# Interleaving the row loads of the next batch with the DMA transposes of the present one

## The chip, the cores and the metric

The kernel runs on one core of one Trainium2 chip. The metric is the device time of one execution in microseconds (us), as a median of several runs. A run over 1.5% above the fastest of the same kernel counts as slow, the others as fast, and only fast runs are compared.

Engines are called PE (TensorE), PEld (TensorE's weight loads), DVE (VectorE), ACT (ScalarE), POOL (GpSimd) and SP (SyncE) in the profile. SPq is SyncE's queue of DMA issues. L373 is line 373 of the kernel's source; most operations go through one helper, so the tile names tell more than the line numbers.

## The reference, cut to what matters

```python
# q, k, v: (8, 8, 576, 64) float32: 8 batches, 8 heads, 576 tokens; s: (8, 8, 576)
scores = (q @ k^T) / 8 + min(-(cum_i - cum_j), 0)      # cum = cumsum(max(s, 0)); causal
x  = softmax(scores) @ v            # -> (4608, 512): 8 heads x 64 are the model dimension
xn = x / sqrt(mean(x^2) + 1e-6) * rms_g
out = (silu(xn @ w_gate) * (xn @ w_val)) @ w_out       # 512 -> 1536 -> 512
```

q and k are drawn as 0.1 × normal. A dot product of 64 terms is then about 0.1 × 0.1 × 8 = 0.08, and a score about 0.01.

## The kernel before

The work goes in nine chunks `c` of 512 tokens. In chunk c, TensorE does the first two FFN products (12 groups of 4 matmuls each with `wg_sb` and `wv_sb`), the attention of batch b = c + 1, and the last FFN product (48 matmuls with `wout_sb`, 10.4 us). Meanwhile rows of K, Q and V for batch c + 2 are loaded.

From batch 2 on, K and Q take this way: a row load of 128 tokens × 8 heads × 64 (256 KB) into `k_nat` or `q_nat`, a cast to bf16 on VectorE (`k_bf`, `q_bf`), and a DMA transpose into `KT` or `QT`. `k_nat`, `q_nat`, `v_nat`, `k_bf` and `q_bf` exist once. SyncE issues the row loads, the transposes, and the stores of the output, all in one queue, in order.

The order on every engine is decided when the kernel is built, by a list scheduler inside it (`Plan`). Each operation has a key (smaller goes first), a planned duration and its dependences. A DMA also has planned times for its transfer. Nothing of this runs on the chip; but every constant in it can move instructions. The loads are held back by one rule:

```python
# Plan.schedule(): when may operation o start on engine e?
can = []
for r, o in cand:                      # r: when its inputs are ready, in planned time
    # ... [cut: PSUM banks, the DMAs of GpSimd]
    if o.dma and e == "sp":
        r = max(r, self.dma_free - 3.0)    # at most 3 us of planned DMA work ahead, from ALL queues
    can.append((o.key, o.n, r, o))
# ... [cut: the candidate with the smallest key among those ready goes next]
if o.dma:
    begin = max(self.dma_free, s + o.us + o.lags[0])
    self.dma_free = begin + o.dma
    o.done = self.dma_free + o.lags[1]
```

The loads, the casts with the transposes, the output, and the loop that gives the keys:

```python
def load_rows(dst, src, b, eng, key):
    ops = []
    for sc in range(NB):               # NB = 5 blocks of 128 tokens, the last of 64
        n = 128 if sc < 4 else 64
        ops.append(I(eng, "dma_start", 0.88 if eng == "pool" else 0.4, key=key,
                     dma=1.28 * n / 128, lags=(1.2, 1.2 if b < 2 else 4.2),
                     out=dst[0:n, sc], in_=src[b, :, sc * 128 : sc * 128 + n, :].rearrange(
                         "h p d -> p h d")))
    return ops

def prep_cast(b, which, key):
    src, dst = ((k_nat, k_bf), (q_nat, q_bf))[which]
    out = (KT, QT)[which][b % 2]
    for sc in range(NB):
        n = 128 if sc < 4 else 64
        I("dve", "tensor_copy", 0.34, key=key + sc, out=dst[0:n, sc], in_=src[0:n, sc])
        I("sp", "dma_start_transpose", 1.27, key=key + sc, dma=0.65, lags=(0.5, 2.7),
          out=out[:, :, sc * 128 : sc * 128 + n], in_=dst[0:n, sc])

# in ffn2(c): O is the finished PSUM bank, osb a ring of NOSB = 3 buffers
    o = nxt("osb", osb)
    I("act", "activation", 0.6, ..., out=o, in_=O, func=AF.Copy, scale=0.5)
    I("sp", "dma_start", 0.4, key=key, dma=0.72, out=out[...], in_=o)

for c in range(NCH):
    K = PER * c                        # PER = 36
    # ... [cut: FFN1 groups of chunk c]
    b = c + 1
    # ... [cut: batches 0 and 1 take another way]
        for w in range(2):
            prep_cast(b, w, K - 14)
    # ...
    if b + 1 < B:
        n = b + 1
        for o in load_rows(k_nat, k, n, "sp", K + 16) + load_rows(q_nat, q, n, "sp", K + 16):
            ...
        lv = load_rows(v_nat[n % len(v_nat)], v, n, "sp", K + 16)
    ffn2(c, K + STEP * 96, STEP)
    attention(b, K + 1, 2.6, 2 if b > 3 else 4)
```

So one batch of loads stands in SyncE's order as five K, five Q and five V, with no transpose between them. `x_blk`, the normed output of attention, is also transposed by DMA (into `xnT`) from batch 3 on.

Of the kernel before, what the change touches and what calls it, by code (L numbers as in the profile page):

```python
# [75 lines left out]
class Plan:  # L76
# [59 lines left out]
    def schedule(self):  # L136
        ops = self.ops
        for o in ops:
            o.succ = []
        left = {}  # L140
        for o in ops:
            left[o.n] = len(o.preds)
            for p in o.preds:
                ops[p].succ.append(o)
        free = {}
        table = {}
        pool = {}
        self.dma_free = 0.0
        order = []
        held = [[0.0, None] for _ in self.banks]  # L150

        def ready(o):
            t = 0.0
            for p, raw in o.preds.items():
                q = ops[p]
                if q.eng == o.eng and not q.dma:
                    t = max(t, q.done if raw and o.eng != "pe" else q.start)
                else:
                    t = max(t, q.done + self.HOP)
            return t  # L160

        def room(o):
            group, cap, n = o.takes[0].group, o.takes[0].cap, len(o.takes)
            for t in sorted(f for f, _ in held if f is not None):
                free = sum(1 for f, _ in held if f is not None and f <= t)
                busy = sum(1 for f, g in held if g == group and (f is None or f > t))
                if free >= n and busy + n <= cap:
                    return t
            return None

        lanes = [0.0] * self.LANES

        def add(o):
            pool.setdefault(o.eng, []).append((ready(o), o))

        for o in ops:
            if not left[o.n]:
                add(o)
        while any(pool.values()):
            best = None  # L180
            for e, cand in pool.items():
                f = free.get(e, 0.8)
                can = []
                for r, o in cand:
                    if o.takes:
                        t = room(o)
                        if t is None:
                            continue
                        r = max(r, t)
                    if o.dma and e == "pool":  # L190
                        r = max(r, lanes[0] + self.HOP)
                    if o.dma and e == "sp":
                        r = max(r, self.dma_free - 3.0)
                    can.append((o.key, o.n, r, o))
                if not can:
                    continue
                t = max(f, min(x[2] for x in can))
                k = min((x for x in can if x[2] <= t + 0.02), key=lambda x: x[:2])
                if e in ("dve", "act", "pool"):
                    soon = [x for x in can if x[:2] < k[:2] and x[2] < t + self.AHEAD * k[3].us]  # L200
                    if soon:
                        k = min(soon, key=lambda x: x[2])
                s = max(f, k[2])
                if best is None or s < best[0]:
                    best = (s, e, k[3], f)
            s, e, o, f = best
            pool[e] = [(r, q) for r, q in pool[e] if q is not o]
            o.wait = s - f
            if o.kind is not None:
                if table.get(e) not in (None, o.kind):  # L210
                    s += self.TABLE
                table[e] = o.kind
            o.start = s
            free[e] = s + o.us
            o.done = s + o.us + o.lat
            if o.dma:
                begin = max(self.dma_free, s + o.us + o.lags[0])
                self.dma_free = begin + o.dma
                o.done = self.dma_free + o.lags[1]
                if e == "pool":  # L220
                    lanes[:] = lanes[1:] + [o.done]
            for bank in o.takes:
                i = min((i for i, (t, _) in enumerate(held) if t is not None),
                        key=lambda i: held[i][0])
                bank.phys = i
                held[i][:] = [None, bank.group]
            for bank in o.uses:
                bank.left -= 1
                if not bank.left:
                    held[bank.phys][0] = max(u.done for u in bank.users) + self.HOP  # L230
            order.append(o)
            for q in o.succ:
                left[q.n] -= 1
                if not left[q.n]:
                    add(q)
        assert len(order) == len(ops)
        self.order = order
        return order
# [7 lines left out]
def kernel(  # L246
# [25 lines left out]
    NB = 5  # L272
# [10 lines left out]
    NS = 3  # L283
    NOSB = 3
    NRUN = 2
    NTWO = 2
    NPE = 3

# [101 lines left out]
    def small_bank():  # L390
        return bank("small", 2)
# [6 lines left out]

    def load_runs(b, which, h0, h1, key):
        p0 = KP * which  # L400
        return I("pool", "dma_start", 0.8, key=key, dma=(4.0, 3.45)[b] * (h1 - h0) / 8, lags=(0.9, 1.3),
                 out=raw[b][p0 : p0 + KP, h0:h1, :, :].rearrange("p h c d -> p h (c d)"),
                 in_=(k, q)[which][b, h0:h1, :, :].rearrange("h (p c) d -> p h (c d)", c=KC))

    def load_rows(dst, src, b, eng, key):
        ops = []
        for sc in range(NB):
            n = 128 if sc < 4 else 64
            ops.append(I(eng, "dma_start", 0.88 if eng == "pool" else 0.4, key=key,
                         dma=1.28 * n / 128,  # L410
                         lags=(1.2, 1.2 if b < 2 else 4.2),
                         out=dst[0:n, sc], in_=src[b, :, sc * 128 : sc * 128 + n, :].rearrange(
                             "h p d -> p h d")))
        return ops

    def load_w(which, lo, hi, key):
        if which == 2:
            return I("pool", "dma_start", 0.84, key=key, dma=9.6 * (hi - lo) / 12,
                     out=wout_sb[:, lo:hi, :],
                     in_=moe_w_out[lo * 128 : hi * 128, :].rearrange("(fc p) d -> p fc d", p=128))  # L420
        dst, src = ((wg_sb, moe_w_gate), (wv_sb, moe_w_val))[which]
        return I("pool", "dma_start", 0.76, key=key, dma=8.9 * (hi - lo) / DF,
                 out=dst[:, :, lo:hi],
                 in_=src[:, lo:hi].rearrange("(cc p) f -> p cc f", p=128))

# [11 lines left out]
        else:  # L437
            I("act", "activation", 0.57, key=key, out=o, in_=i, func=AF.Copy)

    def prep_cast(b, which, key):  # L440
        src, dst = ((k_nat, k_bf), (q_nat, q_bf))[which]
        out = (KT, QT)[which][b % 2]
        for sc in range(NB):
            n = 128 if sc < 4 else 64
            I("dve", "tensor_copy", 0.34, key=key + sc, out=dst[0:n, sc], in_=src[0:n, sc])
            I("sp", "dma_start_transpose", 1.27, key=key + sc, dma=0.65, lags=(0.5, 2.7),
              out=out[:, :, sc * 128 : sc * 128 + n], in_=dst[0:n, sc])

    def prep_norm(b, which, i, key):
        n = 128 if i < 2 else 64  # L450
# [156 lines left out]
    def att_out(b, tb, key):  # L607
        x = x_blk[b % 2][:, tb, :]
        if b >= NPE:
# [1 line left out]
            I("dve", "scalar_tensor_tensor", 0.66, key=key, out=x, in0=x,  # L611
              scalar=al[b % 2][:, 1, tb : tb + 1], in1=gB, op0=ALU.mult, op1=ALU.mult)
            c0 = b * S + tb * 128
            I("sp", "dma_start_transpose", 1.27, key=key - 3, dma=0.65, lags=(0.5, 2.7),
              out=xnT[:, :, c0 : c0 + 128 - p0], in_=x_blk[b % 2][p0:128, tb, :])
            return
        I("act", "activation", 0.5, key=key, out=x, in_=x, func=AF.Copy,
# [51 lines left out]
    def ffn2(c, key, step):  # L669
        t0 = c * DM  # L670
        for tb in range(4):
            O = bank("ffn", 6)
            for f in range(0, FB, 2):
# [3 lines left out]
            o = nxt("osb", osb)  # L677
            I("act", "activation", 0.6, key=key + step * (tb * FB + FB), out=o, in_=O,
              func=AF.Copy, scale=0.5)
            I("sp", "dma_start", 0.4, key=key, dma=0.72,  # L680
              out=out[t0 + tb * 128 : t0 + (tb + 1) * 128, :], in_=o)

    whole = [(0, DM, fb) for fb in range(FB)]
# [36 lines left out]
    for hp in range(HP):  # L720
        prep_transpose(0, 0, hp, -80 + hp, "dve")
        prep_transpose(0, 1, hp, -80 + hp, "act")
    gp_ = small_bank()
    mms(0.1, [(gp_[:, 0:CC], g4, ident_F[0:CC, 0:CC], True, True, True)], key=-75)
    I("dve", "tensor_copy", 0.1, key=-75, out=g_sb, in_=gp_[:, 0:CC])
    prep_w(0, "act", -70)
# [14 lines left out]
    for c in range(NCH):  # L741
# [5 lines left out]
        if b < B:  # L747
# [2 lines left out]
                    prep_transpose(b, 0, hp, K + hp, "dve")  # L750
                    prep_transpose(b, 1, hp, K + hp, "act")
            else:
                for w in range(2):
                    prep_cast(b, w, K - 14)
            if b < NRUN:
                raw_norm(b, K + 18)
            else:
                for i in range(3):
                    for w in range(2):
                        prep_norm(b, w, i, K + 30)  # L760
            prep_w(b, "pool", K - 10)
            vops = [prep_v(b, sc, "pool", K - 8 + sc) for sc in range(NB)]
        if b + 1 < B:
            n = b + 1
            for o in load_rows(k_nat, k, n, "sp", K + 16) + load_rows(q_nat, q, n, "sp", K + 16):
                if n == NRUN:
                    R.after(o, *vops)
            lv = load_rows(v_nat[n % len(v_nat)], v, n, "sp", K + 16)
            if n == NRUN:
                R.after(gl, *lv)  # L770

        if c == B - 1:
            check_decay(K + 10)
            check_all(K + 20)
# [171 lines left out]
```

## Time and profile before

| | before |
|---|---|
| median (range) | 377.04 us (375.39 to 378.92; 3 runs) |
| span of the profiled run | 373.1 us |
| TensorE busy | 341.8 us |
| TensorE idle in 120 to 264 us | 10.94 us |
| one period, first K load to first K load | 39.6 us |

The head of the profile page of the kernel before gives the span, the busy time of each engine (share of the span, instructions) and, in part 4, which engine held the chain of work that ended last:

```profile
span 373.1 us, 7766 instructions
...
PE 341.8 (92%) x2907; PEld 207.6 (56%) x2934; DVE 251.6 (67%) x486; ACT 230.4 (62%) x469; POOL 127.8 (34%) x211
...
PE 62%; DMA 12%; DVE 9%; POOL 5%; SPq 4%; ACT 3%; issue 3%; DVEq 0%; ACTq 0%; POOLq 0%
```

TensorE is the busiest engine, but only 62% of the chain passes over it; a fifth passes over DMA, SyncE's queue and GpSimd. So waits for data are left, and the next question is where. The windows of the kernel before show each stretch of 36 us: its length, the busy time of each engine, the granted clock, the DMA share and the rate in GB/s.

```profile
120.00:156.00 36.00, 33.14 (x302) 23.61 (x301) 26.20 (x48) 22.85 (x49) 15.09 (x23) 0.95 0.89 161
156.00:192.00 36.00, 33.97 (x308) 23.05 (x308) 27.06 (x52) 22.95 (x51) 13.77 (x21) 1.00 0.91 162
192.00:228.00 36.00, 32.92 (x233) 16.19 (x236) 28.20 (x55) 24.02 (x51) 14.22 (x23) 1.00 0.88 163
228.00:264.00 36.00, 33.02 (x236) 16.02 (x240) 28.04 (x54) 22.29 (x48) 14.07 (x21) 1.00 0.85 168
```

TensorE is busy 133.06 of these 144 us. This is the stretch to look at: in the 72 us before it TensorE is idle 1.8 us, and in the 72 us after it 1.2 us. Its waits in this stretch (what it waited for: us in all, times, longest) name two causes:

```profile
PE psb L373 <- DMA QTa<-q_bf: 2.2, 1, 2.2
PE pse L373 <- DVE u_sbc L356: 1.7, 1, 1.7
PE psa L373 <- DVE u_sbc L356: 1.7, 1, 1.7
PE psf L373 <- DMA QTb<-q_bf: 1.6, 1, 1.6
```

Twice TensorE waits for a transpose of Q. Twice it waits for `u_sbc`, an FFN intermediate that VectorE makes. That second wait looks like a slow VectorE and is not. VectorE's timeline of the kernel before (start, duration, instruction, in brackets the idle time before it and its releaser) shows the first of the two:

```profile
209.73 0.66 DVE L356 CAST q_bf<-q_nat 128x512 bf16<-128x512 f32 x1 [1.51 <-DMA q_nat<-in_q_dram]
210.31 0.67 DVE L356 SCALAR_TENSOR_TENSOR u_sbc<-T_sbc,psa 128x512 bf16<-128x512 f32 x1
```

VectorE stood 1.51 us in front of a cast whose row load had not landed, and `u_sbc`, the next in its order, came behind it. TensorE's next matmul then shows 1.74 us idle, put down to `u_sbc`. The other such wait looks the same: VectorE stood 1.30 us in front of a `q_bf` cast at 249.41 us, and `u_sbc` came behind it. Both kinds of wait are therefore late K and Q rows. SyncE's timeline of the kernel before shows why they are late:

```profile
199.57 4.39 SPq L356 DMA_DIRECT2D k_nat<-in_k_dram  x5
204.01 6.49 SPq L356 DMA_DIRECT2D q_nat<-in_q_dram  x5
210.60 5.59 SPq L356 DMA_DIRECT2D v_nata<-in_v_dram  x5
216.28 2.57 SPq L356 DMA_TRANSPOSE xnT<-x_blkb  x2
218.94 1.22 SPq L356 DMA_TRANSPOSE KTa<-k_bf  x1
220.21 1.26 SPq L356 DMA_TRANSPOSE QTa<-q_bf  x1
```

Fifteen loads hold the queue for 16.5 us, 1.1 us each on average, then come the transposes at 1.2 to 1.3 us each. During the loads the share of busy DMA engines was 0.88 to 1.22, during the transposes 0.65 to 0.72. (The share is the time of the packets that start in a stretch over that of 16 engines, so it can pass 1.)

### The profile page before, as it was taken

How to read it: one execution, taken by the hardware profiler on the slowest of the kernel's cores; microseconds unless marked ns; L12 is line 12 of the kernel's file. 1: busy time of each engine (PE TensorE's matmuls, PEld its weight loads, DVE VectorE, ACT ScalarE, POOL GpSimd, SP SyncE). 2: the span in 40 equal slices, each digit the busy share in tenths (PEclk: the TensorE clock that was granted, in tenths of full speed). 3: DMA queues.
4: the chain of work that ended last, by engine and by line, in shares of the span. 5: the costliest groups of instructions: out<-in, count | busy, mean ns of one | idle time of the engine just before them, and what ended most of it. 6: DMA issues, size and time to landing. Idle time of an engine off the chain costs nothing.

```text
span 373.1 us, 7766 instructions
## 1 busy us (share of the span) xinstructions
PE 341.8 (92%) x2907; PEld 207.6 (56%) x2934; DVE 251.6 (67%) x486; ACT 230.4 (62%) x469; POOL 127.8 (34%) x211
## 2 busy tenths in 40 slices
PE   3869999999999997999979799979999999999993
PEld 3558775788577864787435444444445444444441
DVE  6478946797937895588837893879388638806830
ACT  3959698888769825874767547863687533313321
POOL 8976452504361544134613370345123200000000
PEclk9999999999999999899999999999999999999999
DMA  8999997977985997699758986699650170020012
GB/s 125 215 226 208 193 184 164 162 176 153 200 192 116 190 179 132 179 156 198 133 128 183 198 151 115 167 203 174 114 148 2 30 149 0 0 87 29 0 43 78
DMA packets 138356, 51.13 MB, mean 137 GB/s; under 512 B 127300, under 2 KB 132936, under 8 KB 138312
## 3 DMA queue, kind: packets, MB, share of 16 engines
q1 hardware_dynamic: 131688, 41.13, 55.8%
q0 software_dynamic: 6624, 9.44, 14.4%
q8 instruction: 25, 0.41, 0.5%
q14 instruction: 19, 0.16, 0.2%
HBM read 38.16 MB, written 9.44 MB: 128 GB/s over the span
## 4 chain that ended last, share of the span: by engine, by line
PE 62%; DMA 12%; DVE 9%; POOL 5%; SPq 4%; ACT 3%; issue 3%; DVEq 0%; ACTq 0%; POOLq 0%
PE psc L373 9%; PE psb L373 8%; PE psd L373 8%; PE psg L373 8%; PE psh L373 7%; PE psa L373 7%; PE psf L373 7%; PE pse L373 6%; DMA v_nata<-in_v_dram 5%; SPq L356 4%; DVE Hs L356 2%; DMA QTb<-q_bf 2%; DMA out_dram<-osbb 2%; DMA q_nat<-in_q_dram 1%; DMA k_nat<-in_k_dram 1%
## 5 line engine op out<-in xcount | busy, mean ns | idle before, releaser
L373 PEld LDWEIGHTS <-wv_sb 128*128 128x128 bf16 x624 | 60.7, 98 | 39.5 <-issue 7.2
L373 PEld LDWEIGHTS <-wg_sb 128*128 128x128 bf16 x624 | 58.6, 98 | 32.5 <-issue 5.1
L373 PEld LDWEIGHTS <-Hs 128*128 128x128 bf16 x432 | 41.3, 98 | 49.9 <-DVE Hs L356 2.1
L356 POOL TENSOR_TENSOR vwb<-v_nata,wT 128x512 bf16<-128x512 f32 (+1 forms) x20 | 21.1, 1073 | 12.2 <-DMA v_nata<-in_v_dram 11.9
L356 POOL TENSOR_SCALAR_AFFINE_SELECT Ea<-Ea 128x512 bf16<-128x512 bf16 x8 | 5.1, 644 | 56.0 <-ACT Ea L356 56.0
L356 ACT ACTIVATE sq_scr<-x_blka 128x512 bf16<-128x512 bf16 x19 | 12.0, 632 | 15.9 <-DVE x_blka L356 15.6
L356 DVE CAST q_bf<-q_nat 128x512 bf16<-128x512 f32 (+1 forms) x30 | 18.4, 621 | 3.7 <-DMA q_nat<-in_q_dram 3.7
L373 PE MATMUL psf<-xnT,wv_sb 128*128 128x256 bf16 (+1 forms) x116 | 20.6, 313 | 0.2
L356 ACT ACTIVATE sq_scr<-x_blkb 128x512 bf16<-128x512 bf16 x20 | 12.6, 630 | 13.1 <-DVE x_blkb L356 12.6
L356 POOL TENSOR_TENSOR vwa<-v_nata,wT 128x512 bf16<-128x512 f32 (+1 forms) x15 | 16.2, 1094 | 9.5 <-DMA v_nata<-in_v_dram 9.3
L356 DVE CAST k_bf<-k_nat 128x512 bf16<-128x512 f32 (+1 forms) x30 | 15.1, 515 | 5.2 <-DMA k_nat<-in_k_dram 5.2
L373 PE MATMUL psc<-wout_sb,Hs 128*128 128x512 bf16 x69 | 17.0, 379 | 0.9 <-DVE Hs L356 0.7
L373 PE MATMUL psd<-xnT,wg_sb 128*128 128x256 bf16 (+1 forms) x95 | 17.5, 316 | 0.1
L373 PE MATMUL pse<-xnT,wg_sb 128*128 128x256 bf16 (+1 forms) x102 | 17.3, 304 | 0.1
L373 PE MATMUL psh<-wout_sb,Hs 128*128 128x512 bf16 x70 | 16.6, 379 | 0.5 <-DVE Hs L356 0.4
L373 PE MATMUL psg<-wout_sb,Hs 128*128 128x512 bf16 x70 | 16.6, 379 | 0.1
L356 ACT ACTIVATE sq_scr<-q_bf 128x1024 bf16<-128x1024 bf16 (+1 forms) x18 | 16.5, 916 | 0.2
L373 PE MATMUL psc<-xnT,wg_sb 128*128 128x256 bf16 (+1 forms) x83 | 14.9, 316 | 1.8 <-DVE xnT L356 1.5
L373 PE MATMUL psb<-xnT,wg_sb 128*128 128x256 bf16 (+1 forms) x95 | 16.3, 308 | 0.1
L356 ACT ACTIVATE sq_scr<-k_bf 128x1024 bf16<-128x1024 bf16 (+1 forms) x18 | 16.3, 908 | 0.0
L356 DVE SCALAR_TENSOR_TENSOR x_blkb<-x_blkb,alb,gB 128x512 bf16<-128x512 bf16 x15 | 12.1, 859 | 5.0 <-POOL alb L356 5.0
L373 PE MATMUL psa<-xnT,wv_sb 128*128 128x256 bf16 (+1 forms) x75 | 13.4, 311 | 1.9 <-DVE u_sbc L356 1.7
(456 smaller groups left out, 859.6 us busy)
## 6 DMA issues: line engine op xcount, KB each, us to landing
k_nat<-in_k_dram SPq DMA_DIRECT2D x24, 256.0 KB, 4.7
q_nat<-in_q_dram SPq DMA_DIRECT2D x24, 256.0 KB, 5.8
v_nata<-in_v_dram SPq DMA_DIRECT2D x24, 256.0 KB, 5.1
out_dram<-osba SPq DMA_DIRECT2D x12, 256.0 KB, 2.3
out_dram<-osbb SPq DMA_DIRECT2D x12, 256.0 KB, 2.4
out_dram<-osbc SPq DMA_DIRECT2D x12, 256.0 KB, 2.4
v_nata<-in_v_dram POOLq DMA_DIRECT2D x8, 256.0 KB, 11.0
wg_sb<-in_moe_w_gate_dram POOLq DMA_DIRECT2D x2, 768.0 KB, 12.9
```

The costliest lines, as they stand in the source:

```text
L356: o = R.add(eng, us, lambda: f(**{n: real(a) for n, a in kw.items()}), outs, ins, key=key, lat=LAT[eng], kind=kind, dma=dma, name=outs[0]. ...
L373: nc.tensor.matmul(out, lhsT=lhsT, rhs=rhs, start=st, stop=sp)
```

## The change

The intent is to spread the loads: the pair of loads of K and Q for block sc of the next batch gets the key of the transposes of block sc + LEAD of the present one. By then the casts of block sc have freed that part of `k_nat` and `q_nat`. DMA engines then have loads to move while SyncE issues transposes. V follows after. The rule that holds back SyncE's DMAs now looks at SyncE's own DMAs only. The planned durations were measured again. The core of the diff:

```diff
@@ Plan.schedule
+        sp_free = 0.0
                     if o.dma and e == "sp":
-                        r = max(r, self.dma_free - 3.0)
+                        r = max(r, sp_free - 2.0)
 ...
+                if e == "sp":
+                    sp_free = self.dma_free
@@ constants
+    LEAD = 1
+    MARGIN = 3.0
-dma=(4.0, 3.45)[b] ... 0.4, dma=1.28 * n / 128      (row loads: issue, transfer)
+dma=(3.95, 3.35)[b] ... 0.45, dma=1.2 * n / 128
-dma=9.6 ... dma=8.9                                 (weights)
+dma=8.0 ... dma=7.8
-"dma_start_transpose", 1.27 ... "dma_start", 0.4, dma=0.72   (transposes, output stores)
+"dma_start_transpose", 1.31 ... "dma_start", 0.62, dma=0.75
@@ prep_cast: K and Q of one block together
-    for sc in range(NB):
-        (cast, transpose of one tensor; called for K, then for Q)
+    for sc in range(NB):
+        for src, dst, out in ((k_nat, k_bf, KT[b % 2]), (q_nat, q_bf, QT[b % 2])):
+            (cast, transpose)
@@ main loop
-            for o in load_rows(k_nat, k, n, "sp", K + 16) + load_rows(q_nat, q, n, "sp", K + 16):
-                if n == NRUN:
-                    R.after(o, *vops)
-            lv = load_rows(v_nat[n % len(v_nat)], v, n, "sp", K + 16)
+            K2 = K - 14 + LEAD
+            for sc in range(NB):
+                for dst, src in ((k_nat, k), (q_nat, q)):
+                    o = load_row(dst, src, n, sc, "sp", K2 + sc)
+                    if n == NRUN:
+                        R.after(o, *vops)
+            lv = [load_row(v_nat[n % len(v_nat)], v, n, sc, "sp", K2 + 6 + sc) for sc in range(NB)]
 ... [cut: prep_norm's keys, K + 30 -> K + 20 + 2 * i; another PSUM group for one small transpose]
```

(The lines of constants are abridged: the numbers are those of the diff, the code around them is left out.)

More of the change, by code (lines that the diff above doesn't have):

```diff
@@ L400, in load_runs, with load_row @@
         p0 = KP * which
-        return I("pool", "dma_start", 0.8, key=key, dma=(4.0, 3.45)[b] * (h1 - h0) / 8, lags=(0.9, 1.3),
+        return I("pool", "dma_start", 0.8, key=key, dma=(3.95, 3.35)[b] * (h1 - h0) / 8, lags=(0.9, 1.3),
                  out=raw[b][p0 : p0 + KP, h0:h1, :, :].rearrange("p h c d -> p h (c d)"),
                  in_=(k, q)[which][b, h0:h1, :, :].rearrange("h (p c) d -> p h (c d)", c=KC))
-    def load_rows(dst, src, b, eng, key):
-        ops = []
-        for sc in range(NB):
-            n = 128 if sc < 4 else 64
-            ops.append(I(eng, "dma_start", 0.88 if eng == "pool" else 0.4, key=key,
-                         dma=1.28 * n / 128,
-                         lags=(1.2, 1.2 if b < 2 else 4.2),
-                         out=dst[0:n, sc], in_=src[b, :, sc * 128 : sc * 128 + n, :].rearrange(
-                             "h p d -> p h d")))
-        return ops
+    def load_row(dst, src, b, sc, eng, key):
+        n = 128 if sc < 4 else 64
+        return I(eng, "dma_start", 0.88 if eng == "pool" else 0.45, key=key, dma=(1.08 if eng == "pool" else 1.2) * n / 128,
+                 lags=(1.2, 1.2 if b < NRUN else MARGIN + 1.2), out=dst[0:n, sc],
+                 in_=src[b, :, sc * 128 : sc * 128 + n, :].rearrange("h p d -> p h d"))
+    def load_rows(dst, src, b, eng, key):
+        return [load_row(dst, src, b, sc, eng, key) for sc in range(NB)]
     def load_w(which, lo, hi, key):
         if which == 2:
-            return I("pool", "dma_start", 0.84, key=key, dma=9.6 * (hi - lo) / 12,
+            return I("pool", "dma_start", 0.84, key=key, dma=8.0 * (hi - lo) / 12,
                      out=wout_sb[:, lo:hi, :],
@@ L421, in load_w @@
         dst, src = ((wg_sb, moe_w_gate), (wv_sb, moe_w_val))[which]
-        return I("pool", "dma_start", 0.76, key=key, dma=8.9 * (hi - lo) / DF,
+        return I("pool", "dma_start", 0.76, key=key, dma=7.8 * (hi - lo) / DF,
                  out=dst[:, :, lo:hi],
@@ L438, in prep_transpose, with prep_cast @@
             I("act", "activation", 0.57, key=key, out=o, in_=i, func=AF.Copy)
-    def prep_cast(b, which, key):
-        src, dst = ((k_nat, k_bf), (q_nat, q_bf))[which]
-        out = (KT, QT)[which][b % 2]
+    def prep_cast(b, key):
         for sc in range(NB):
             n = 128 if sc < 4 else 64
-            I("dve", "tensor_copy", 0.34, key=key + sc, out=dst[0:n, sc], in_=src[0:n, sc])
-            I("sp", "dma_start_transpose", 1.27, key=key + sc, dma=0.65, lags=(0.5, 2.7),
-              out=out[:, :, sc * 128 : sc * 128 + n], in_=dst[0:n, sc])
+            for src, dst, out in ((k_nat, k_bf, KT[b % 2]), (q_nat, q_bf, QT[b % 2])):
+                I("dve", "tensor_copy", 0.34, key=key + sc, out=dst[0:n, sc], in_=src[0:n, sc])
+                I("sp", "dma_start_transpose", 1.31, key=key + sc, dma=0.65,
+                  lags=(0.5, 0.9 + 0.6 * MARGIN),
+                  out=out[:, :, sc * 128 : sc * 128 + n], in_=dst[0:n, sc])
     def prep_norm(b, which, i, key):
@@ L613, in att_out @@
             c0 = b * S + tb * 128
-            I("sp", "dma_start_transpose", 1.27, key=key - 3, dma=0.65, lags=(0.5, 2.7),
+            I("sp", "dma_start_transpose", 1.31, key=key - 3, dma=0.65, lags=(0.5, 0.9 + 0.6 * MARGIN),
               out=xnT[:, :, c0 : c0 + 128 - p0], in_=x_blk[b % 2][p0:128, tb, :])
@@ L679, in ffn2 @@
               func=AF.Copy, scale=0.5)
-            I("sp", "dma_start", 0.4, key=key, dma=0.72,
+            I("sp", "dma_start", 0.62, key=key, dma=0.75,
               out=out[t0 + tb * 128 : t0 + (tb + 1) * 128, :], in_=o)
@@ L722 @@
         prep_transpose(0, 1, hp, -80 + hp, "act")
-    gp_ = small_bank()
+    gp_ = bank("g", 1)
     mms(0.1, [(gp_[:, 0:CC], g4, ident_F[0:CC, 0:CC], True, True, True)], key=-75)
@@ L752 @@
             else:
-                for w in range(2):
-                    prep_cast(b, w, K - 14)
+                prep_cast(b, K - 14)
             if b < NRUN:
@@ L759 @@
                     for w in range(2):
-                        prep_norm(b, w, i, K + 30)
+                        prep_norm(b, w, i, K + 20 + 2 * i)
             prep_w(b, "pool", K - 10)
```

## The prediction

> **What bounds it now.** TensorE: 341.8 of 373.1 us busy, 62% of the chain of waits. In the middle, batches 3 to 6, a second loop is as long: SyncE's queue. The timeline of SyncE shows the five K loads starting at 120.36, 160.01, 199.57 and 239.18 us: one batch takes 39.6 us, with hardly a gap. At 199.57 to 239.18 it spends 16.5 us on 15 row loads (back to back[...]), 19 us on 15 transposes (1.22 to 1.27 us each) and 2 to 3 us on output stores. TensorE is busy only 36.4 to 37.3 us of those 39.6 (windows by batch). DMA engines are loaded unevenly: share 0.88 to 1.22 while rows load, 0.65 to 0.72 while transposes go.
>
> TensorE's idle time in 120–264 us is 11.0 us. Its waits name the cause: 2.2 and 1.6 us for the transposes of Q at 147 and 188; twice 1.7 us for u_sb at 209 and 249. The second kind is also late loads: just before, VectorE stands 1.5 us in front of a cast that waits for a q_nat load, with u_sb behind it. GpSimd waits 3.6 us for v_nata at 212. After the 2.2 us stall some matmul groups take 1.6 to 1.9 us, not 1.04: 1.4 us more.
>
> **What the change does.** Same bytes, same transfers, same arithmetic. A pair of row loads follows the transposes of its block, so DMA fills the time in which SyncE issues transposes (two take 2.5 us), and the solid 11 us of K and Q loads ahead of V disappears. Issue of a load without a wait is about 0.4 us; one batch should hold SyncE about 15×1.26 + 15×0.45 + 2.5 = 28 us instead of 39.6 (estimate from these durations). V starts right after the last transpose instead of 11 us later. Casts spread out in VectorE's order. The new constants of the planner also move part of attention later, into the second FFN matmul of some chunks.
>
> The Trainium skill ("DMA: Bandwidth & Descriptors", Issuing engines are not separate DMA queues) says that all DMAs end on the same 16 engines and interleave. So bandwidth isn't gained: about 0.87×39.6 = 34.5 us of DMA work stays per batch. At a 37.5 us period that is a share of 0.92, so landings of transposes should lengthen, from 2.5 us to perhaps 3.5, and part of the gain goes back.
>
> **On the critical path.** Removable: 11.0 us of idle in 120–264, plus 1.4 us of slow clock. I expect about two thirds: 8.5 us. Start (11 us idle before 48, from first loads and set-up), 48–120 (1.9 us idle) and the last 75 us (FFN alone, store tail) stay within 1 us. 377.0 − 8.5 = **368.5 us**, range **362 to 376**. Faster by over 2%: 0.55; within 2%: 0.41; slower: 0.04.
>
> **Right if:** TensorE's busy time stays near 340 to 343 while its idle in 120–264 falls from 11 to 3–5 us; the period of K loads falls to about 37 to 38 us; waits of TensorE on the Q transposes and of VectorE on q_nat (3.5 us) nearly vanish; SyncE has free time in each batch; DMA share is even, about 0.9; transposes land later than 2.5 us.
>
> **Wrong if:** DMA is the true limit of the middle and the period stays at 39; or in-order SyncE now makes a transpose wait behind a load whose buffer isn't free, so attention starts late; or the moved attention leaves xnT late at the start of a chunk (waits of TensorE on xnT, DVE x_blk); or the new order of the first 60 us costs some us.

## The result, and the profile after

The ratios in this document are the mean time of one kernel's fast runs over that of the other's of the same rounds, so they are not quite the ratio of the medians quoted beside them.

| | before | after |
|---|---|---|
| median (range), same chip | 376.86 us (375.39 to 378.92; 4 runs) | 363.19 us (362.05 to 363.79; 4 runs) |
| ratio, 95% interval | | 0.963 (0.958 to 0.968): faster |
| span of the profiled run | 373.1 us | 360.4 us |
| TensorE busy | 341.8 us | 340.6 us |
| TensorE idle in 120 to 264 us | 10.94 us | 2.19 us |
| period in this stretch (before: first K load to first K load; after: first V load to first V load) | 39.6 us | 37.9 to 38.3 us |

The gain of the medians is 13.7 us. The head of the page and the chain by engine of the kernel after:

```profile
span 360.4 us, 7813 instructions
...
PE 340.6 (95%) x2934; PEld 207.1 (57%) x2934; DVE 251.3 (70%) x486; ACT 230.9 (64%) x469; POOL 129.0 (36%) x211
...
PE 76%; DVE 10%; ACT 4%; POOL 3%; DMA 3%; issue 2%; SPq 0%; DVEq 0%; ACTq 0%; POOLq 0%
```

The work is the same, but DMA fell from 12% to 3% of the chain and SyncE's queue from 4% to 0%. The windows of the kernel after, same columns as before:

```profile
120.00:156.00 36.00, 34.85 (x340) 25.70 (x339) 28.47 (x57) 28.35 (x62) 15.79 (x24) 1.00 0.97 175
156.00:192.00 36.00, 35.97 (x295) 22.64 (x294) 28.59 (x53) 24.00 (x52) 13.41 (x21) 1.00 0.93 163
192.00:228.00 36.00, 35.32 (x267) 17.16 (x265) 27.80 (x56) 24.11 (x51) 14.52 (x24) 1.00 0.96 173
228.00:264.00 36.00, 35.67 (x250) 17.06 (x249) 27.82 (x52) 25.27 (x53) 15.04 (x21) 1.00 0.74 147
```

TensorE is busy 141.81 of 144 us. The longest two waits of TensorE in this stretch after the change show that no transpose and no long `u_sb` wait is left:

```profile
PE psh L378 <- DVE x_blkb L361: 0.7, 1, 0.7
PE psa L378 <- DVE u_sba L361: 0.4, 1, 0.4
```

SyncE's timeline of the kernel after shows the pairs between the transposes:

```profile
210.38 1.22 SPq L361 DMA_TRANSPOSE KTa<-k_bf  x1
211.65 1.26 SPq L361 DMA_TRANSPOSE QTa<-q_bf  x1
212.96 0.58 SPq L361 DMA_DIRECT2D k_nat<-in_k_dram  x1
213.59 0.57 SPq L361 DMA_DIRECT2D q_nat<-in_q_dram  x1
214.26 0.78 SPq L361 DMA_DIRECT2D out_dram<-osbb  x1
215.14 1.24 SPq L361 DMA_TRANSPOSE KTa<-k_bf  x1
```

These loads hold SyncE for 0.57 us each, where in the block five loads of Q held it for 6.49 us. Not all are so short: from 115 to 270 us the loads of K and Q hold it for 0.58 us in the median (0.42 to 1.85), before for 0.86 us (K) and 1.10 us (Q). The price stands in the list of DMA issues of the kernel after (out<-in, queue, operation, count, median us from issue to landing):

```profile
KTa<-k_bf SPq DMA_TRANSPOSE x15, 3.6
QTa<-q_bf SPq DMA_TRANSPOSE x15, 2.7
```

Before, both stood at 2.5 us. The loads themselves land sooner: K 3.6 us (before 4.7), Q 4.2 (before 5.8); V lands in 5.7 (before 5.1).

So loads no longer reach TensorE. But the change did two things at once. It changed SyncE's order, and through keys, rule and constants it also made the planner put TensorE's, VectorE's and ScalarE's instructions in another order. TensorE's order in the program shows it. G and V are FFN1 groups, s scores, a products with V, O the last FFN product, with the number of matmuls; chunk 4, at its start:

```
before:  G4 V4 s8 G4 V4 G4 V4 a6 G4 V4 s8 a6 ...                              O48
after:   G4 V4 G4 V4 G4 V4 G4 V4 G4 s8 V4 ... G4 V4 O6 s12 O12 a12 O4 a12 O26
```

Before, the first scores of the batch stand after one FFN1 group; after, they stand after four and a half, and the last ones stand inside the last FFN product. Chunk 4 moves farthest. In chunk 5 the first scores stand after one and a half groups, in chunk 3 only later ones have moved, and chunk 6, whose batch has no loads between its transposes, has the order of before. Which of the two pays is what the experiments had to settle.

### The profile page after: what moved, and what is told of

It is laid out like the page before. It is cut to its first block, busy times and chain, and to the rows that moved or that the text cites. A ratio compares the mean times of both kernels' runs of the same rounds, so it can differ in the third digit from the quotient of the medians.

```text
span 360.4 us, 7813 instructions
## 1 busy us (share of the span) xinstructions
PE 340.6 (95%) x2934; PEld 207.1 (57%) x2934; DVE 251.3 (70%) x486; ACT 230.9 (64%) x469; POOL 129.0 (36%) x211
## 4 chain that ended last, share of the span: by engine, by line
PE 76%; DVE 10%; ACT 4%; POOL 3%; DMA 3%; issue 2%; SPq 0%; DVEq 0%; ACTq 0%; POOLq 0%
PE psb L378 10%; PE psa L378 10%; PE psf L378 10%; PE psg L378 9%; PE psh L378 9%; PE psc L378 9%; PE psd L378 9%; PE pse L378 9%; DVE Hs L361 2%; DVE x_blkb L361 2%; DMA q_nat<-in_k_dram 1%; DMA v_nata<-in_v_dram 1%; DVE u_sbb L361 1%; DVE u_sbc L361 1%; DVE u_sba L361 1%
## 5 line engine op out<-in xcount | busy, mean ns | idle before, releaser
L361 ACT ACTIVATE sq_scr<-x_blka 128x512 bf16<-128x512 bf16 x19 | 12.0, 629 | 13.1 <-DVE x_blka L361 12.7
L378 PE MATMUL psb<-wout_sb,Hs 128*128 128x512 bf16 x84 | 19.8, 379 | 0.0
L378 PE MATMUL psc<-xnT,wv_sb 128*128 128x256 bf16 (+1 forms) x104 | 16.6, 297 | 0.0
L378 PE MATMUL psa<-xnT,wg_sb 128*128 128x256 bf16 (+1 forms) x96 | 16.5, 308 | 0.0
L378 PE MATMUL psh<-xnT,wg_sb 128*128 128x256 bf16 (+1 forms) x100 | 16.5, 302 | 0.0
L361 DVE CAST q_bf<-q_nat 128x512 bf16<-128x512 f32 (+1 forms) x30 | 15.8, 526 | 0.6 <-DMA q_nat<-in_q_dram 0.6
L361 POOL TENSOR_TENSOR vwa<-v_nata,wT 128x512 bf16<-128x512 f32 (+1 forms) x15 | 15.3, 1038 | 1.4 <-DMA v_nata<-in_v_dram 1.3
L378 PE MATMUL psd<-xnT,wv_sb 128*128 128x256 bf16 (+1 forms) x84 | 15.5, 318 | 0.0
L378 PE MATMUL psg<-xnT,wg_sb 128*128 128x256 bf16 (+1 forms) x72 | 14.2, 335 | 1.1 <-DVE xnT L361 1.1
L378 PE MATMUL psa<-xnT,wv_sb 128*128 128x256 bf16 (+1 forms) x84 | 15.0, 317 | 0.0
L378 PE MATMUL psd<-wout_sb,Hs 128*128 128x512 bf16 x60 | 14.3, 379 | 0.3 <-DVE Hs L361 0.3
L378 PE MATMUL psf<-wout_sb,Hs 128*128 128x512 bf16 x60 | 14.6, 379 | 0.0
```

The costliest lines, as they stand in the source:

```text
L361: o = R.add(eng, us, lambda: f(**{n: real(a) for n, a in kw.items()}), outs, ins, key=key, lat=LAT[eng], kind=kind, dma=dma, name=outs[0]. ...
L378: nc.tensor.matmul(out, lhsT=lhsT, rhs=rhs, start=st, stop=sp)
```

## The experiments

The theories:

- **A**: SyncE's order alone pays. The new place of attention is a side effect.
- **B**: the planner's new order of compute pays.
- **C**: where an interleaved version gains little, its output stores have been pushed back in SyncE's queue, and a fourth output buffer gives the gain back. **D** is its rival: the transposes and casts are late, and a fourth buffer only uncovers that. **E** extends C to the kernel before.
- **F**: interleaving spreads the ten transposes of a batch over a longer time, so the last ones land later; attention must stand later in TensorE's order to profit. **G** is its rival, for which the place of attention matters little.

Two methods are used. "Frozen" kernels let the planner make its plan, then move only the DMA issues named, and leave the order on all other engines; a comparison of the instruction streams confirmed it. "Re-planned" kernels change an input of the planner and take what comes out. The kernels of one set ran on one chip with kernel before beside them: set 1 (before: 376.22 us, 7 runs) are the first four below, set 2 (377.36 us, 7 runs) the next four, set 3 (376.21 us, 7 runs) the last four. Across sets, ratios to before are the better measure.

### b_inter: SyncE's order alone, in the kernel before

Frozen. The order on TensorE, VectorE, ScalarE and GpSimd has no difference to before.

```diff
+        for n in range(3, 8):                       # after the plan is made
+            mine = [load[w, n, sc] for sc in range(5) for w in "kq"]
+            order = [o for o in order if o not in mine]
+            for o in reversed(mine):                # behind both transposes of block sc + 1 of batch n - 1
+                i = max(order.index(transpose[w, n - 1, min(o.sc + 1, 4)]) for w in "kq")
+                order.insert(i + 1, o)
```

> The kernel before with its planned order frozen; only on SyncE are the K and Q row loads of batches 3 to 7 moved, a pair behind the transposes of the block one further on. TensorE, VectorE, ScalarE and GpSimd keep before's order exactly. Theory A (the order on SyncE is what pays, because transposes' issue time hides the loads): most of the gain is here, 363 to 368 us, TensorE idle in 120-264 us from 11 to 4 or less, K-load period about 37 us. Rival B (the planner's new constants moved attention and casts to better places on the compute engines): within 1% of before, 373 to 377 us, because the waits of TensorE come from the compute order.

Measured: 370.39 us (368.54 to 373.89), ratio 0.985 (0.977 to 0.993): a gain of 5.8 us, clear of 1 but not of the 2% line, so the verdict is unclear. TensorE's idle time in 120 to 264 us is 7.41 us, against 10.94. SyncE's order alone gives less than half of 13.7 us. The waits that are left are for the output buffers (1.8, 1.7 and 0.8 us) and a Q transpose (1.2 us).

### a_block: the new order of compute alone, with the loads back in a block

Frozen, from the kernel after. The loads go back in front of V; about twenty casts that would then precede their load are put off behind it on VectorE, and this is the one difference on the compute engines.

```diff
+        for n in range(3, 8):
+            mine = [load[w, n, sc] for w in "kq" for sc in range(5)]
+            order = [o for o in order if o not in mine]
+            i = order.index(load["v", n, 0])
+            order[i:i] = mine
+        # an operation whose inputs are not there yet is put off until they are (only casts)
```

> The changed kernel with its order frozen; on SyncE the ten K and Q row loads of batches 3 to 7 stand in one block ahead of the V loads, as before; the 20 casts that this would put ahead of their load are moved just behind it on VectorE, all else keeps its order. Theory A: the time goes back by most of the gain, to 371 to 377 us, or above, as the compute order was planned for early loads. Rival B: 363 to 366 us, since the compute order is kept.

Measured: 387.85 us (387.61 to 390.11), ratio 1.031 (1.026 to 1.037): slower than before by 11.6 us. TensorE's idle time in the stretch is 15.11 us, and its granted clock in those windows 0.95 to 0.97. TensorE's longest waits from 84 to 264 us in this kernel:

```profile
PE psa L418 <- DVE Hs L401: 4.2, 1, 4.2
PE pse L418 <- DVE u_sba L401: 3.9, 1, 3.9
PE psc L418 <- DVE x_blka L401: 3.4, 1, 3.4
```

They are all waits for VectorE, which from 84 to 264 us stands 13.7 us, in ten waits, in front of casts of `q_nat`. So the new order of compute cannot live with the old order of loads. Frozen, the four corners are:

| | loads in a block | loads interleaved |
|---|---|---|
| compute order of before | 376.2 (before) | 370.4 (b_inter) |
| compute order of after | 387.9 (a_block) | 363.2 (after, another chip) |

A and B, each alone, fall: interleaving gives 5.8 us in the old compute order and 24.7 us (across two chips) in the new one.

### plan_block: after's planner, with the load code of before

Re-planned, with the new rule and constants.

```diff
-            K2 = K - 14 + LEAD
-            for sc in range(NB): ... (pairs, then V)
+            for dst, src in ((k_nat, k), (q_nat, q)):
+                for o in load_rows(dst, src, n, "sp", K + 16): ...
+            lv = load_rows(v_nat[n % len(v_nat)], v, n, "sp", K + 16)
```

> The changed kernel with only the row loads handed to the planner as before (five K, five Q, five V with one late key); all new constants, the new rule for SyncE, the paired transposes and the bank of the small transpose stay, and the planner plans anew. Theory A: 372 to 378 us, close to before. Rival B: 363 to 367 us.

Measured: 369.54 us (368.34 to 370.95), ratio 0.981 (0.975 to 0.987), a gain of 6.7 us that is clear of 1 but not of the 2% line, so the verdict is unclear; idle in the stretch 5.96 us. The planner's part pays about as much as b_inter's when it may fit compute to the block. The longest wait that it leaves in the stretch is the first kind of before's. It stands in front of the first scores of chunk 4, where this plan has TensorE's order of before; in chunks 5 and 6 it puts the first scores after five and a half and six groups:

```profile
PE psc L378 <- DMA QTb<-q_bf: 3.4, 1, 3.4
```

### keys_only: the kernel before with the interleaved keys and nothing else

Re-planned, with the old rule and the old constants.

```diff
-            (K and Q: load_rows with key K + 16; V: key K + 16)
+            K2 = K - 14 + 1
+            (pairs K, Q with key K2 + sc; V with key K2 + 6 + sc)
```

> The kernel before with only the keys of the row loads changed (pairs of K and Q loads, block by block, V after them); all of the old constants and the old rule for SyncE stay, and the planner plans anew. Theory A: 362 to 367 us, the gain is had without the new constants. Rival B: 371 to 377 us.

Measured: 377.52 us (375.52 to 379.22), ratio 1.004 (0.997 to 1.010): the same as before. Idle in the stretch is 10.87 us. The very edit that gives the change its name moves nothing if the planner is left as it was. TensorE's longest waits in it:

```profile
PE psc L373 <- ACT osba L356: 3.9, 1, 3.9
PE pse L373 <- ACT osbb L356: 2.5, 1, 2.5
```

They are new, and before has none of over 0.4 us of this kind. ScalarE's timeline of keys_only shows the one at 194 us:

```profile
194.08 0.60 ACT L356 ACTIVATE osba<-psc 128x512 f32<-128x512 f32 x1 [5.63 <-DMA out_dram<-osba]
```

ScalarE stood 5.63 us because an output buffer had not been stored yet. Theory C came from this line.

### keys_osb4: keys_only with a fourth output buffer

The order on all engines is that of keys_only; the plan is made with three buffers, and the program uses a ring of four.

```diff
-    NOSB = 3
+    NOSB = 4            # planned with osb[0:3], emitted with all four
```

> The kernel in which only the keys of the row loads were changed (377.5 us, no gain), in the same order on every engine, but with four output buffers in place of three, so that the fourth ScalarE copy of a chunk need not wait for its first store. Theory C (interleaving alone pushes the output stores back in SyncE's queue; ScalarE, in order, stands before the fourth copy, up to 5.6 us, and TensorE's next FFN groups behind it, 3.9, 2.5 and 1.1 us): the time falls by about these 7.5 us, to 368 to 371 us, and the waits of TensorE on osb vanish. Rival D (the waits on osb only stand in front of other lateness of the same order): 374 to 378 us, other waits take their place.

Measured: 375.52 us (372.63 to 378.15), ratio 0.997 (0.992 to 1.002): the same as before. Idle in the stretch is 9.76 us, against 10.87, which is no more than the scatter of this figure (b_osb4, below). The waits for output buffers are gone from the top of the list; a Q transpose (2.6 us) and `u_sba` (1.4, 1.2 and 1.1 us) have taken their place. That fits D: the stores were the wait that ended last, with the next one hidden right behind it.

### b_inter_osb4: b_inter with a fourth output buffer

> Before's frozen order with interleaved loads (370.4 us), with four output buffers. Theory C: its 4.3 us of waits of TensorE on osb go, 365 to 367.5 us. Rival D: 369 to 371 us.

Measured: 369.96 us (365.16 to 371.71; the highest run was slow), ratio 0.973 (0.965 to 0.981); idle in the stretch 6.74 us, against 7.41. The runs scatter, the interval overlaps b_inter's, and the difference is unclear. TensorE's waits in the stretch:

```profile
PE psa L391 <- DMA QTa<-q_bf: 2.6, 1, 2.6
PE psd L391 <- DMA QTa<-q_bf: 2.3, 1, 2.3
PE psb L391 <- DMA QTb<-q_bf: 0.8, 1, 0.8
```

With the stores out of the way, the three longest waits are all for Q transposes: 5.7 us in all. D again, and more purely than in keys_osb4.

### b_osb4 and a_osb4: a fourth buffer in before and in after

The controls, with the same edit.

> The kernel before in the same order with four output buffers. Its trace has 13 us of waits of ScalarE for output stores, but only 0.5 us of TensorE named after osb. Theory C: stores are a small part of before's loss, 373 to 376 us. A third theory (E: the stores are the main loss of before, and loads matter only through them): 363 to 369 us.

> The changed kernel in the same order with four output buffers. No wait of TensorE on osb is left in its trace. Theory C and rival D both: 362 to 364 us; if it gains more than 1.5 us, stores still cost in the changed kernel.

Measured: b_osb4 376.05 us (374.09 to 378.08), ratio 0.998 (0.992 to 1.003), idle in the stretch 12.23 us: the same as before, so E falls. a_osb4 362.5 us (361.94 to 364.14), ratio 0.960 (0.956 to 0.965), idle 3.83 us: no clear difference to after, whose ratio was 0.963 (0.958 to 0.968). The fourth buffer is worth nothing by itself in either. The controls also show how far one profiled run's idle time scatters in the same order of instructions: 10.94 and 12.23 us in before's, 2.19 and 3.83 us in after's.

### b_inter_osb4_late3: half of the attention later in TensorE's order

This is the test of F. Why should transposes be late if loads are early? From the start of the first to the end of the last issue of the ten K and Q transposes of a batch, SyncE's timelines give, for batches 2 to 7:

```
before    16.2  16.4  19.8  20.0  20.2  20.3 us
b_inter   21.6  21.6  24.3  25.2  25.4  20.0 us
after     21.4  21.3  29.7  25.5  28.3  19.7 us
```

The loads stand between the transposes now, so the last transpose of a batch comes some 5 us (in after up to 10 us) later after the first one than before, and TensorE in b_inter asks for it at the old place. The edit moves the second half of the heads (scores, products with V, norm) of batches 3 to 7 later by 3 in keys, about one and a half FFN1 groups. The planner of before makes the plan anew, which moves instructions on the other engines too, and then the loads are moved as in b_inter.

```diff
+        late = [0 if u < HP else 3 for u in range(2 * HP)]      # for b >= 3
-            unit_av(b, u, key + step * (u + 1.5), Es)
+            unit_av(b, u, key + late[u] + step * (u + 1.5), Es)  # the same for scores and the norm
```

> Before's planner with four output buffers, the second half of the attention of batches 3 to 7 (scores, products with V, normalisation) given a key that is later by 3, which is one and a half FFN groups in TensorE's order, and then the K and Q loads interleaved on SyncE as in the runs before. To be compared with the same kernel without the later key (370.0 us), whose trace has waits of TensorE of 1.8, 2.3, 0.8 and 2.6 us in front of second-half scores, for the transposes of Q. Theory F (interleaving spreads a batch's ten transposes over more time, so that their last ones land later, and attention has to stand later in TensorE's order to gain from it): these waits vanish, 362 to 366 us. Rival G (the order of attention does not matter, DMA bandwidth is short whatever the order): 368 to 372 us.

Measured: 365.55 us (363.2 to 368.92; the highest run was slow), ratio 0.969 (0.964 to 0.974): faster than before. Idle in the stretch fell from 6.74 to 3.05 us. TensorE's longest waits in it:

```profile
PE psh L391 <- DVE Hs L374: 1.3, 2, 0.9
PE psa L391 <- DVE u_sbc L374: 0.8, 1, 0.8
```

The 5.7 us of waits for Q transposes are gone. A fourth one, which the expectation counted as well, stays: 1.84 us at 94.8 us in b_inter_osb4, 1.65 us at 93.5 us here. It lies before the stretch, in batch 2, whose attention the edit leaves in its place. In time the interval overlaps that of b_inter_osb4 (0.965 to 0.981), so the gain of the later attention in time is not certain; that these waits vanish is what the trace shows. Against b_inter (0.977 to 0.993), later attention and the fourth buffer together are a clear gain. The result lies near after, without after's rule and constants.

### a_oldrule: after, with one line of the planner as before

Re-planned.

```diff
-                        r = max(r, sp_free - 2.0)
+                        r = max(r, self.dma_free - 3.0)
```

> The changed kernel with the old rule for SyncE in the planner (a DMA may be issued 3 us before the planned end of all DMA, in place of 2 us before that of SyncE's own). Loads stay interleaved, all else stays; but the plan has attention early again in chunks 2 to 6, as before. Theory F: a large part of the gain goes, 368 to 374 us, with waits of TensorE for Q transposes or output buffers. If 363 to 365 us, the place of attention does not matter.

Measured: 376.16 us (373.61 to 379.9; the highest run was slow), ratio 0.995 (0.991 to 1.000): the same as before. One line of the planner takes away all of the gain. Idle in the stretch is 9.16 us. The order on TensorE is changed with it: in chunks 3 to 6 the first scores stand after one FFN1 group, as in before (in chunk 2 too, where before has four groups). The rule also changes the order on SyncE, so this run does not move attention alone. TensorE's longest waits in the stretch:

```profile
PE psc L378 <- ACT osbc L361: 3.9, 1, 3.9
PE psa L378 <- ACT osba L361: 3.8, 1, 3.8
```

They have keys_only's form. SyncE's timeline of a_oldrule shows the store that the second one needed:

```profile
189.72 3.73 SPq L361 DMA_DIRECT2D v_nata<-in_v_dram  x3
193.55 1.57 SPq L361 DMA_DIRECT2D out_dram<-osba  x1
```

ScalarE had filled this buffer at 185.14 us; its store was issued at 193.55 us, behind loads; and ScalarE's timeline shows the bill:

```profile
198.33 0.60 ACT L361 ACTIVATE osba<-psa 128x512 f32<-128x512 f32 x1 [6.09 <-DMA out_dram<-osba]
```

A wait of this length costs twice. TensorE's timeline of a_oldrule right after it:

```profile
198.98 1.87 PE L378 MATMUL psa<-xnT,wv_sb 128*128 128x512 bf16 x4 [3.76 <-ACT osba L361]
200.63 1.82 PE L378 MATMUL pse<-xnT,wg_sb 128*128 128x512 bf16 x4
202.29 1.03 PE L378 MATMUL psb<-xnT,wv_sb 128*128 128x512 bf16 x4
```

Two groups of four matmuls take 1.87 and 1.82 us where the next takes 1.03: the clock had fallen (0.50 was granted from 199 to 202 us) and came back. Over the run TensorE's busy time is 346.1 us for the same matmuls, 5.5 us more than after's; its trace has three such stretches of 3.4 us. The Trainium skill ("TensorE: Matmul & The Clock Gate", HAM oscillation) warns of just this for idle gaps over about 3.4 us; the 3.76 us here agree.

### a_oldconst: after, with all planned durations of before and the new rule

Re-planned.

```diff
-(3.95, 3.35); 0.45, 1.2; 8.0; 7.8; 1.31; 0.62, 0.75
+(4.0, 3.45);  0.4, 1.28; 9.6; 8.9; 1.27; 0.4, 0.72
```

> The changed kernel with all durations of DMA and issue in the planner as before, but with the new rule for SyncE and interleaved loads. The plan has attention even later than the changed kernel, from the fourth to seventh FFN group on. Theory F: the gain stays, 361 to 366 us. If 370 us or more, it is the new durations that matter, not the place of attention.

Measured: 363.44 us (362.53 to 365.51), ratio 0.965 (0.962 to 0.968): the full gain. Idle in the stretch 2.23 us. The constants that were measured again do nothing for the time. In chunk 4 this plan puts attention even later than after's: the first scores after seven groups. The re-planned kernels now make a table:

| load keys | rule | constants | median | ratio to before |
|---|---|---|---|---|
| block | old | old | 376.2 (before) | 1 |
| interleaved | old | old | 377.5 (keys_only) | 1.004 |
| interleaved | old | new | 376.2 (a_oldrule) | 0.995 |
| block | new | new | 369.5 (plan_block) | 0.981 |
| interleaved | new | old | 363.4 (a_oldconst) | 0.965 |
| interleaved | new | new | 363.2 (after) | 0.963 |

### b_noload: before without the K and Q loads of batches 3 to 7

Frozen; 50 loads are left out. The computation is wrong: those batches use stale rows. The comparison with the reference passed all the same, because scores are about 0.01 here; that pass says nothing about the kernel being right.

```diff
+        gone = [load[w, n, sc] for n in range(3, 8) for w in "kq" for sc in range(5)]
+        order = [o for o in order if o not in gone]
```

> The kernel before in its frozen order, with the 50 K and Q row loads of batches 3 to 7 taken out (batch 2's rows are used again: a wrong result on purpose). Theory A (these loads in SyncE's queue and on the DMA engines are what makes before's transposes late): 361 to 367 us, with TensorE's idle in 120-264 us below 4. If it stays above 371 us, before's loss lies in its compute order and not in the loads.

Measured: 360.8 us (360.38 to 361.1), ratio 0.959 (0.956 to 0.962). One of its windows, same columns as before:

```profile
156.00:192.00 36.00, 36.00 (x316) 23.23 (x314) 28.62 (x55) 26.36 (x55) 14.74 (x24) 1.00 0.55 116
```

TensorE has no idle time at all here, and 0.44 us in the whole stretch. So the K and Q loads are behind nearly all of before's 10.94 us. The run takes away their place in SyncE's queue and their DMA traffic together. But after moves the same bytes as before and, with all loads in place, is within 2.4 us (by the medians, on another chip) of a kernel that doesn't have these 50, so bandwidth alone was not what held before back.

## Why the prediction was right or wrong

**The result.** Predicted 368.5 us, range 362 to 376, faster most likely. Measured 363.19: faster, inside the range, near its lower end. The gain was 13.7 us, and 8.5 us had been predicted. That it lies in the range is in part luck. The step on which the prediction built, SyncE's new order, gives 5.8 us when it is made alone (b_inter); the rest needed the planner's move of attention, which the prediction feared.

**What bounds the kernel: right.** TensorE's busy time stayed (341.8 to 340.6 us; 340 to 343 was predicted), and the idle time in the middle was the K and Q loads': b_noload takes 10.94 down to 0.44 us. Reading the `u_sbc` waits as late loads was right too. V's rows were also late: from 115 to 270 us GpSimd stood 16.2 us in front of operations on `v_nata` before, and 3.8 us after. They don't decide the time: these waits are gone in b_inter, which gains 5.8 us, and 15.3 us long in plan_block, which gains 6.7 us. VectorE's waits over the whole run fell from 3.7 to 0.6 us for `q_nat` and from 5.2 to 0.0 for `k_nat`, TensorE's for Q transposes from 4.1 us to none.

**The period: nearly right.** 37 to 38 us was predicted for K loads. The first K loads of three batches start at 136.56, 174.78 and 212.96 us, 38.2 us apart; from the first V load of a batch to the next it is 38.3, 37.9 and 38.3 us.

**DMA: right.** The Trainium skill ("DMA: Bandwidth & Descriptors", Issuing engines are not separate DMA queues) says that all DMAs run on the same 16 engines and interleave. The trace agrees: the same bytes moved, and the share by period rose from between 0.86 and 0.88 to between 0.93 and 0.95 as the period got shorter. The landings of transposes grew less evenly than predicted (2.5 to 3.5 us): those of K from 2.5 to 3.0 and 3.6 us, those of Q only to 2.6 and 2.7 us.

**The sizes: too small.** The prediction's sum was "about two thirds" of 11.0 us of idle and 1.4 us of slow clock, 8.5 us, with the rest "within 1 us". Of the idle in 120 to 264 us came 10.94 - 2.19 = 8.75 us, which is 80%, and busy time fell by 1.2 us: 9.95 us together. The rest gave 2.7 us: 1.1 in 48 to 120, 1.1 in 264 to 300, and 0.5 at the start. These make up the 12.7 us by which the spans differ. The medians differ by 1.0 us more, because before's profiled run lay 2.1 us under its median and after's 1.1 us. So of the 5.2 us missed, 1.5 lie in the factor two thirds, 2.7 in the parts held to be unmoved, and 1.0 in the run profiled.

**"SyncE has free time in each batch": wrong.** 28 us of 39.6 was estimated. In the trace SyncE's queue is occupied 36.4 of 38.3 us after, against 38.0 of 39.6 before. The step that failed was adding up issue times as if an entry lasted only as long as its issue. The 0.4 us for a load is 0.58 us in the median, and other entries stretch by waiting: one batch of V loads took 6.9 us. Yet the queue is no longer what binds: TensorE is busy 37.15 of 38.30, 37.91 of 37.94 and 37.60 of 38.28 us. Occupancy of an in-order queue is no measure of what it needs.

**"The new constants of the planner also move part of attention later": half right, and undervalued.** Attention does move later. But a_oldconst shows that it isn't the constants, and a_oldrule that it is the rule. And the prediction took this for a side effect that might hurt ("the moved attention leaves xnT late"). About half of the gain hangs on it: without it, interleaving brings 5.8 us (b_inter) or nothing (keys_only).

**What the experiments support.** The loads between the transposes get K and Q rows to VectorE in time and stretch a batch's transposes by some 5 to 10 us, so the last ones land later. Attention at its old place then waits for them. This is F. For it speak the vanishing of 5.7 us of waits for Q transposes in b_inter_osb4_late3, the gain kept in a_oldconst with attention later still, and the gain lost in a_oldrule with attention early. C, the stores, falls as the cause in keys_only and b_inter: a fourth buffer takes those waits away, and the next ones take their place.

**What stays open.** In a_oldrule the waits that show are those of the stores, not of the transposes, so it speaks for F only together with keys_osb4. In time, b_inter_osb4_late3 and b_inter_osb4 overlap, and the first is planned anew, so more than attention differs. Later attention with the loads left in their block, in before's planner, was not run. Why 3 us of all planned DMA against 2 us of SyncE's own moves the plan so far was not taken apart; no kernel with keys and rule and nothing else was run, though a_oldconst comes close to it. Other values of LEAD were not run.

## What to carry to other kernels

When one queue in order carries loads and transposes, put each load behind the operation that frees its buffer, and then move the consumers of the transposes later by as much as the transposes have been stretched: here either step alone gave 7 us or less (frozen, the new order of compute alone even cost 11.6 us), and both together 13.7. Where a wait names a compute engine, look at what that engine itself stood in front of. A wait that ends last may hide another just behind it, so take it away in an experiment before calling it the cause.

## What the Trainium skill lacked or had wrong

- "DMA: Bandwidth & Descriptors", Issuing engines are not separate DMA queues, says that the sequencer time to start a DMA "is usually small relative to the DMA itself". For transposes it is not small here: a 128x512 bf16 transpose held SyncE 1.22 to 1.26 us of the 2.5 us to its landing, and 15 of them some 19 us of a batch of 39.6 us.
- The same page has no time to landing for a transpose of this size from SBUF to SBUF on this chip, nor what it costs beside row loads: the runs show 2.5 us to landing in before, where loads and transposes stand apart, and 2.6 to 3.6 us for K and Q in after, where they are interleaved. Its Rules for kernel authors say that a transpose next to ordinary DMAs needs nothing; the correct results of all runs with right data agree, but it costs landing time.
- No page looked up warns that a store stands behind loads in one engine's queue of issues ("Perfetto Trace Analysis", Sequencer Loop, lists reading the next instruction, pushing it into the engine's queue, and its waits for semaphores and resources). The runs show ScalarE held for 6.09 us (a_oldrule) and 5.63 us (keys_only) by such a store.
- "TensorE: Matmul & The Clock Gate", HAM oscillation, puts the gap that makes the clock fall at about 3.4 us. After 48 us of each trace, all seven gaps of 3.35 us or more come with a fall, but a shorter one can be enough. In the kernel before, a fall followed one of 2.21 us: 0.50 was granted from 151.0 to 153.5 us, and a group of eight matmuls of 256 columns took 1.87 us, where about 1.0 is usual. In b_osb4, with the same order, the clock stayed at 1.00 after a gap of 2.23 us at the same place. Of the other gaps of 2.0 to 2.9 us, a fall came with those of 2.08 (a_oldrule), 2.34 (b_inter_osb4), 2.62 (keys_osb4) and 2.87 us (a_block), and none with those of 2.49 (keys_only) and 2.55 us (b_inter_osb4). The two gaps of 1.7 us in before had no fall behind them.
- No page looked up says that the time an issue holds SyncE depends on what is already under way: in the block of ten at 199.57 us (before) the first two loads held it 0.57 and 0.58 us and the other eight 0.62 to 2.42 us; between transposes (after) a Q load held it 0.58 us in the median.
